# A fused attention and two-layer mixture kernel: the first block multiplies unsplit float32, the weights are split behind it, and the list scheduler models VectorE and GpSimd as alternating

## The chip, the core and the metric

The kernel runs on one core of a Trainium2 chip. The metric is device microseconds of one execution. The kernel before takes 977.46 us (median of 3 runs, 977.22 to 979.46).

## The reference

Three stages follow one another, with 4 sequences of 768 steps (3072 tokens of 384 channels, 8 heads of 48).

```python
# 1: gated linear attention, a recurrence over time with a complex decay
scale = np.minimum(mag, 0.999) / (mag + 1e-06)      # mag = |a|
new_re = ar * S_re - ai * S_im;  new_im = ar * S_im + ai * S_re
S_re, S_im = new_re + k[t] v[t]^T, new_im;  y[t] = q[t] @ S_re
# 2: x = (x @ w_a) * (x @ w_b) @ w_out              384 -> 1536 -> 384
# 3: the best of 8 experts per token: out = gate * (relu(x @ w1[e]) @ w2[e])
```

The weights `w_a`, `w_b` and `w_out` of stage 2 are stored as float64, 36 pieces of 128 x 384 values.

## The kernel before

The first two stages run over 12 blocks of 256 tokens, each with two halves c of 128. For a block, `pre` turns the decay into factors on k and q (elementwise on VectorE, ScalarE and GpSimd; DMAs then turn them into `kT` and `qT`), `attn` computes scores, mask, y and the running state with fp32 products, and `planned_moe` does stage 2. The experts of stage 3 follow in program order after block 11.

Stage 2 works in three passes of fp32r: each operand is split into a high part H (ScalarE's copy, which rounds) and a remainder L (a subtraction), and a product is the sum of H*H, H*L and L*H. For one of 12 slices f of 128 inner channels, `up(j, f)` does 18 matmuls of 256 columns into `ab_p`; `gate_a` and `gate_b` multiply both halves into `g`; `gate_H` (ScalarE) and `gate_L` (GpSimd) split it; `down(j, f)` adds six matmuls of 392 columns to `o` (384 channels and 8 gate columns that were folded into `w_out`: `turned`, `kept`, `folded`). `close` empties `o`, `store` writes it to memory.

Each piece of weights is unpacked by `conv`: a DMA loads 384 KB of float64 words; three integer operations on VectorE (`shift` L771, `low` L774, `sign` L777) put an fp32 value together from both words in `ca`; ScalarE makes H (`high` L784), GpSimd the remainder (`rest` L788). A load waits for the unpacking six pieces before (`AHEAD`). Blocks 0 and 1 need the weights while they are still being unpacked, so their stage 2 is cut in halves: block 0 with f 0 to 5, block 1 with f 0 to 5, block 0 with f 6 to 11, block 1 with f 6 to 11 (`HALVES`); the first half of each is kept in SBUF (`part`, `keep`) and added by `close`.

The order of all instructions of this part is the work of a list scheduler, `Plan`. `P.add` takes an engine, a duration (from `on`), what is read and written, and a due time `at`. `P.run` walks in model time: among the operations that could start first, the one with the lowest due time is issued. So a due time is a priority, and the engines then run their queues in the order written. The due times are in `PRE` (elementwise work of each block), `ATT`, `CONV` (start and step of the unpacking), `HALVES` and `SLOT` (49 for each later block). Which elementwise products go to GpSimd is in `ON_POOL`, by block (3 stands for all later ones). Before the change the model delays only a VectorE operation marked `fast`, and only behind a GpSimd operation. `spans` (in blocks 3 to 11, four pieces each) loads the weights again and checks their range.

Of the kernel before, what the change touches and what calls it, by code (L numbers as in the profile page):

```python
# [24 lines left out]
AHEAD = 6  # L25
# [265 lines left out]
class Plan:  # L291
# [5 lines left out]
    def add(self, engine, weight, f, r=(), w=(), at=0.0, take=None, give=None, size=0, fast=False, early=0.0, soft=None):  # L297
# [13 lines left out]
        self.ops.append(dict(e=engine, d=weight, f=f, at=at, need=need, take=take, give=give, size=size, fast=fast, early=early, soft=soft, n=n))  # L311
        return n

    def run(self):
# [13 lines left out]
        gone, pipe, port, out, sent = {}, 0.0, (0.0, 0.0), [], [0.0] * 8  # L328
        while any(open_.values()):
# [75 lines left out]
def fast(tc, q, k, v, a_re, a_im, w_a, w_b, w_out, w_gate, w1, w2, out, dram, x2d):  # L405
# [5 lines left out]
    with ExitStack() as mctx, ExitStack() as ctx:  # L411
# [89 lines left out]
        def spans(i, src, nm, f, at):  # L501
# [3 lines left out]
            def load():  # L505
                raw = G["r"] = cvp.tile([128, 2, DM + NE], U32, tag="part", name="ck", bufs=2).rearrange("p h n -> p (h n)")[:, 0:768].rearrange("p (n two) -> p n two", two=2)
# [8 lines left out]
            P.add("SP", 0.06, load, w=[("part", i % 2)], at=at, size=393, early=at)  # L515
            for n, op in enumerate((ALU.max, ALU.min)):
                P.add("DVE", on("DVE", 384), reduce(n, op), r=[("part", i % 2)], w=[("span", i, n)], at=at + 6)
# [230 lines left out]
        three = cvp.tile([128, 1], U32, name="three")  # L748
        nc.vector.memset(three, 3)

        def conv(i, f, src, nm, at):
# [4 lines left out]
            ca, bits = ("x2", i % 5) if x2 else ("ca", i % 5 if i % 5 else 2), ("bits", i)  # L756

            def load():
                raw = wts.tile([128, 768], U32, tag=f"w{nm}{f}", name="raw")
                if nm == "o":  # L760
                    d = nc.sync.dma_start(out=raw, in_=src[f * 128:(f + 1) * 128].bitcast(U32))
                else:
                    d = nc.sync.dma_start(out=raw.rearrange("p (k n) -> p k n", k=3), in_=src.bitcast(U32)[:, f * 256:(f + 1) * 256].rearrange("(k p) n -> p k n", p=128))
# [3 lines left out]
                K["lo"], K["hi"] = raw[:, :, 0], raw[:, :, 1]  # L767
# [8 lines left out]
            def sign():  # L776
                r = nc.vector.scalar_tensor_tensor(out=K["a"], in0=K["hi"], scalar=0xC0000000, in1=K["a"], op0=ALU.bitwise_and, op1=ALU.bitwise_or)  # L777
                unpacked[i] = getattr(r, "ins", r).name
                K["a"] = K["a"].bitcast(F32)
# [142 lines left out]
        def planned_moe(j, f0, f1, lo, hi, on_pool):  # L922
# [6 lines left out]
            def falls(f, at):  # L929
                P.add("PE", 1.08, lambda: down(j, f, f0, f1 - 1), r=[("gH", base + f), ("gL", base + f), ("W", "o", f), ("G", f)], w=["o0", "o1"], at=at)  # L930
                if f < f1 - 1:
                    return
# [498 lines left out]
```

## Time and profile before

| | kernel before |
|---|---|
| median of the runs | 977.46 us |
| the profiled execution | 977.4 us |
| its span (first to last instruction) | 975.6 us |
| mean granted clock of TensorE | 0.972 |
| TensorE, VectorE, ScalarE, GpSimd busy | 890.0, 632.1, 441.4, 383.3 us |

The page gives busy times over the whole span; the windows view cuts the span into stretches and gives for each the busy time of every engine and the granted clock. The lines view groups instructions by line and shape, with busy time and mean duration, and what ended the idle time before them. The timeline lists single instructions with their start. PE is TensorE, DVE is VectorE, ACT is ScalarE, POOL is GpSimd, SP issues the DMAs. Neighbouring rows of one engine overlap by up to about 0.1 us; the time from start to start is what an instruction costs its queue.

### The profile page before, as it was taken

What the parts mean: (1) busy time and instruction counts of PE and PEld (TensorE: products, weight loads), DVE (VectorE), ACT (ScalarE), POOL (GpSimd) and SP (SyncE); (2) the same over time, 40 slices, a digit from 0 to 9 for tenths busy, and PEclk for the clock granted to TensorE, in tenths of its full rate; (3) what the DMA queues carried; (4) which work ended last, traced back from release to release, by engine and by line L of the source; (5) the groups of instructions that cost most, each with busy time, mean ns of one, the idle gap of its engine ahead of it and who ended that gap; (6) DMA issues with size and microseconds to landing.
All of it is one profiled execution on the core that took longest, in us unless ns stands there. A gap on an engine that the chain in (4) does not pass through costs nothing. (4 is left out here: it accounts for less than half of the span.)

```text
span 975.6 us, 19062 instructions
## 1 busy us (share of the span) xinstructions
PE 890.0 (91%) x7404; PEld 863.2 (88%) x7404; DVE 632.1 (65%) x1222; ACT 441.4 (45%) x824; POOL 383.3 (39%) x364
## 2 busy tenths in 40 slices
PE   0467896898999999999999999999999999999994
PEld 0357886898999999999999999999999999999994
DVE  6988999696958585858585959433573455444540
ACT  5445444554645555545454545222443444343430
POOL 3634555633334343334343434121415363342411
PEclk9999698799999999999999999999999999999997
DMA  8561742337261625161626161302334354443611
GB/s 223 160 173 51 212 119 66 82 108 198 64 197 45 187 65 164 42 187 42 180 55 180 26 171 26 99 2 77 120 106 137 109 174 125 150 150 110 178 38 23
DMA packets 128897, 112.72 MB, mean 116 GB/s; under 512 B 36564, under 2 KB 123446, under 8 KB 128796
## 3 DMA queue, kind: packets, MB, share of 16 engines
q1 hardware_dynamic: 122620, 101.30, 36.7%
q0 software_dynamic: 6176, 10.08, 3.5%
q8 instruction: 61, 1.00, 0.4%
q14 instruction: 40, 0.33, 0.1%
HBM read 82.42 MB, written 10.56 MB: 95 GB/s over the span
## 5 line engine op out<-in xcount | busy, mean ns | idle before, releaser
L854 POOL TENSOR_TENSOR gL<-g,gH 128x256 fp32r<-128x256 f32 x132 | 112.9, 857 | 213.7 <-ACT gH L850 207.5
L838 PE MATMUL ab_p<-xH,wa 128*128 128x256 f32 x864 | 189.3, 295 | 4.9 <-DVE g L846 4.5
L838 PE MATMUL ab_p<-xH,wb 128*128 128x256 f32 x864 | 180.4, 285 | 0.0
L863 PE MATMUL o<-wo,gH 128*128 128x392 f32 x576 | 154.6, 349 | 5.3 <-ACT gH L850 5.3
L838 PEld LDWEIGHTS ab_p<-xH,wa 128*128 128x128 f32 x864 | 147.3, 195 | 9.0 <-DVE g L846 6.1
L838 PEld LDWEIGHTS ab_p<-xH,wb 128*128 128x128 f32 x864 | 146.9, 194 | 0.0
L843 ACT COPY g<-ab_p 128x256 f32<-128x256 f32 x144 | 53.2, 370 | 196.6 <-PE ab_p L838 189.9
L846 DVE TENSOR_TENSOR g<-g,ab_p 128x256 f32<-128x256 f32 x144 | 59.7, 414 | 117.9 <-ACT g L843 117.7
L838 PE MATMUL ab_p<-xL,wa 128*128 128x256 f32 x432 | 123.8, 286 | 2.8 <-DVE xL L1238 2.8
L838 PE MATMUL ab_p<-xL,wb 128*128 128x256 f32 x432 | 123.2, 285 | 0.0
L863 PEld LDWEIGHTS o<-wo,gH 128*128 128x128 f32 x576 | 98.7, 191 | 6.6 <-ACT gH L850 5.7
L863 PE MATMUL o<-wo,gL 128*128 128x392 f32 x288 | 99.9, 347 | 3.3 <-POOL gL L854 3.3
L710 DVE SCALAR_TENSOR_TENSOR hL<-h_p,hH 128x256 fp32r<-128x256 f32 (+5 forms) x80 | 41.3, 517 | 90.6 <-ACT hH L709 90.3
L838 PEld LDWEIGHTS ab_p<-xL,wa 128*128 128x128 f32 x432 | 84.4, 195 | 3.0 <-DVE xL L1238 3.0
L709 ACT ACTIVATE hH<-h_p 128x256 fp32r<-128x256 f32 (+5 forms) x80 | 36.7, 459 | 110.5 <-PE h_p L705 109.9
L838 PEld LDWEIGHTS ab_p<-xL,wb 128*128 128x128 f32 x432 | 84.0, 194 | 0.0
L850 ACT ACTIVATE gH<-g 128x256 fp32r<-128x256 f32 x144 | 59.5, 414 | 51.8 <-DVE g L846 51.7
L723 PE MATMUL o<-w2H,hH 128*128 128x384 f32 (+4 forms) x232 | 79.1, 341 | 0.0
L723 PE MATMUL o<-w2H,hL 128*128 128x384 f32 (+4 forms) x232 | 78.5, 338 | 0.0
L723 PE MATMUL o<-w2L,hH 128*128 128x384 f32 (+4 forms) x232 | 78.3, 338 | 0.0
L705 PE MATMUL h_p<-sH,w1H 128*128 128x256 f32 (+5 forms) x240 | 77.4, 322 | 0.0
L705 PE MATMUL h_p<-sH,w1L 128*128 128x256 f32 (+5 forms) x240 | 76.9, 320 | 0.0
(192 smaller groups left out, 1979.2 us busy)
## 6 DMA issues: line engine op xcount, KB each, us to landing
raw<-in_moe_w_dram SPq DMA_DIRECT2D x64, 384.0 KB, 3.5
q<-in_q_dram SPq DMA_DIRECT2D x24, 192.0 KB, 3.4
v<-in_v_dram SPq DMA_DIRECT2D x24, 192.0 KB, 3.3
raw<-in_moe_w_a_dram SPq DMA_DIRECT2D x12, 384.0 KB, 3.9
raw<-in_moe_w_b_dram SPq DMA_DIRECT2D x12, 384.0 KB, 5.0
raw<-in_moe_w_out_dram SPq DMA_DIRECT2D x12, 384.0 KB, 3.5
x2d<-x SPq DMA_DIRECT2D x24, 192.0 KB, 2.7
ck<-in_moe_w_a_dram SPq DMA_DIRECT2D x12, 384.0 KB, 3.3
```

Of the source, the lines that this page charges most:

```text
L705: nc.tensor.matmul(out=t, lhsT=lh[:, o:o + 128], rhs=rh[:, kk].rearrange("p c t -> p (c t)"), start=n == 0, stop=n == 8)
L709: nc.scalar.activation(out=hH, in_=t, func=ACTF.Relu)
L710: nc.vector.scalar_tensor_tensor(out=hL, in0=t, scalar=0.0, in1=hH.bitcast(F32), op0=ALU.max, op1=ALU.subtract)
L723: nc.tensor.matmul(out=G["o", c], lhsT=lh[:, c * r:(c + 1) * r], rhs=rh, start=f == 0 and n == 0, stop=f == NH - 1 and n == 2)
L838: nc.tensor.matmul(out=t[:, i], lhsT=lh[:, kk * 128:(kk + 1) * 128], rhs=rh[:, kk], start=n == 0, stop=n == 8)
L843: nc.scalar.copy(out=G["g", j, f], in_=G["ab", j, f][:, 0])
L846: nc.vector.tensor_tensor(out=G["g", j, f], in0=G["g", j, f], in1=G["ab", j, f][:, 1], op=ALU.mult)
L850: nc.scalar.activation(out=G["H", j, f], in_=G["g", j, f], func=ACTF.Copy)
L854: eng.tensor_tensor(out=G["L", j, f], in0=G["g", j, f], in1=G["H", j, f].bitcast(F32), op=ALU.subtract)
L863: nc.tensor.matmul(out=G["o", j, c], lhsT=lh[:, c * C:(c + 1) * C], rhs=rh, start=f == first and n == 0, stop=f == last and n == 2)
```

## The change

Block 0 is no longer split. Its attention output is copied as fp32 (`x32`), `up32` multiplies it with the unpacked weights `A32` (6 fp32 matmuls of 256 columns for a slice), the gate is one product without H and L, and `down32` does two fp32 matmuls of 392 columns. `conv` stops after `sign`, which writes the value over the high word of the loaded piece (so values lie two words apart); `shift` is a tensor_scalar with an immediate. `parted` splits the pieces afterwards, with `high` on ScalarE and `rest` on VectorE, due from 84 at steps of 1.2. Each piece is loaded into the place of the tile that the next one's split will take (`follows`), so a split waits until the piece in its place has been split. Blocks 0 and 1 run whole and one after the other (`M0`, `M1`), and `part` is gone; block 1's `gate_L` is on VectorE. Fewer elementwise products are on GpSimd, and where `sq` isn't, the square is on ScalarE. The scheduler's `lock` marks operations of VectorE and GpSimd that take turns: one that would start while the other engine's last is running ends after it by its own duration. `alone=False` exempts those that read PSUM and some others. Loads go 14 pieces ahead, with earliest times in `LOAD`. The range checks are in the last six blocks, six pieces each.

```diff
-AHEAD = 6
+AHEAD = 14
+LOAD = (4.0,2.0,7,30.0,2.0)
...
-PRE = ((0.0, 24.0), (10.0, 34.0), (28.0, 52.0), (100.0, 132.0), (140.0, 176.0))
-ATT = (36.0, 54.0, 124.0, 145.0)
-CONV = (30.0, 2.4)
-HALVES = ((44.0, 72.0), (72.0, 96.0), (96.0, 118.0), (118.0, 138.0))
+PRE = ((0.0, 20.0), (2.0, 22.0), (40.0, 70.0), (100.0, 125.0), (140.0, 166.0))
+ATT = (26,66,110,156)
+CONV = (22,1.8)
+M0 = (40.0, 90.0)
+M1 = 88
+SPLIT = (84,1.2)
...
 ON_POOL = {
     0: ("sq", "add", "imul", "k1", "q1"),
-    1: ("sq", "add", "imul", "kA", "qA", "k1"),
-    2: ("sq", "add", "imul", "kA", "qA", "q1"),
-    3: ("sq", "add", "qA", "q1"),
+    1: ("x",),
+    2: ("qA", "q1"),
+    3: ("add", "qA", "q1"),
 }
+GL_POOL = (2, 12)
+L_POOL = ()
...
-            if o["fast"] and x < port[1]:
-                x = port[1]
             end = x + o["d"]
-            if e == "POOL" and o["d"] > 0.3:
-                port = (x, end)
-            free[e] = end
+            if o["lock"]:
+                if port[0] != e and port[1] > x:
+                    end = port[1] + o["d"] - (0.13 if e == "DVE" else 0.06)
+                port = (e, end)
+            free[e] = end - (0.075 if e == "DVE" and o["d"] > 0.2 else 0.0)
...
-            P.add("SP", 0.06, load, w=[("part", i % 2)], at=at, size=393, early=at)
+            P.add("SP", 0.06, load, w=[("s", "bo"[i % 2], NF)], at=at, size=393, early=at)
...
+        follows = {("a", f): ("b", f) for f in range(NF)}
+        follows.update({("b", f): ("a", f + 1) for f in range(NF - 1)})
+        follows.update({("o", f): ("o", f + 1) for f in range(NF - 1)})
+        A32 = {}
...
+            to = follows.get((nm, f))
+            slot = ("s",) + (to or (nm, NF))
+
+            start = LOAD[0] + LOAD[1] * i if i < LOAD[2] else LOAD[3] + LOAD[4] * (i - LOAD[2])
...
-                raw = wts.tile([128, 768], U32, tag=f"w{nm}{f}", name="raw")
+                raw = wts.tile([128, 2 * n], U32, tag="w%s%d" % to, name="raw") if to else cvp.tile([128, 2 * n], U32, tag="last" + nm, name="raw")
...
+                K["lo"], K["hi"] = raw[:, 0:384, 0], raw[:, 0:384, 1]
+                A32[nm, f] = raw[:, :, 1].bitcast(F32)
...
-                nc.vector.scalar_tensor_tensor(out=K["a"], in0=K["hi"], scalar=0x07FFFFFF, in1=three.to_broadcast([128, 384]), op0=ALU.bitwise_and, op1=ALU.logical_shift_left)
+                nc.vector.tensor_scalar(out=K["a"], in0=K["hi"], scalar1=0x07FFFFFF, scalar2=3, op0=ALU.bitwise_and, op1=ALU.logical_shift_left)
...
-                r = nc.vector.scalar_tensor_tensor(out=K["a"], in0=K["hi"], scalar=0xC0000000, in1=K["a"], op0=ALU.bitwise_and, op1=ALU.bitwise_or)
+                r = nc.vector.scalar_tensor_tensor(out=K["hi"], in0=K["hi"], scalar=0xC0000000, in1=K["a"], op0=ALU.bitwise_and, op1=ALU.bitwise_or)
...
-            def high():
-                w = wts.tile([128, 2, n], F32R, tag=f"w{nm}{f}", name=f"w{nm}{f}")
-                W[nm, f] = w[:, 0], w[:, 1]
-                nc.scalar.activation(out=w[:, 0, 0:384], in_=K["a"], func=ACTF.Copy)
...
-            def rest():
-                wH, wL = W[nm, f]
-                nc.gpsimd.tensor_tensor(out=wL[:, 0:384], in0=K["a"], in1=wH[:, 0:384].bitcast(F32), op=ALU.subtract)
...
-            P.add("SP", 0.06, load, r=[("bits", i - AHEAD)], w=[("raw", i)], at=at - 14, size=393)
-            P.add("DVE", on("DVE", 384), shift, r=[("raw", i)], w=[ca, "next"], at=at)
-            P.add("DVE", on("DVE", 384), low, r=[("raw", i), ca], w=[ca], at=at)
-            P.add("DVE", on("DVE", 384), sign, r=[("raw", i)], w=[ca, bits], at=at)
-            P.add("ACT", on("ACT", 384), high, r=[ca], w=[("H", nm, f)], at=at)
-            P.add("POOL", on("POOL", 384), rest, r=[ca, ("H", nm, f)], w=[("W", nm, f)], at=at)
+
+            P.add("SP", 0.06, load, r=[("bits", i - AHEAD)], w=[slot], at=start, early=start, size=393)
+            P.add("DVE", on("DVE", 384, fast=True), shift, r=[slot], w=[ca], at=at)
+            P.add("DVE", on("DVE", 384), low, r=[slot, ca], w=[ca], at=at)
+            P.add("DVE", on("DVE", 384), sign, r=[ca], w=[slot, bits, ("A32", nm, f)], at=at)
...
+            def beside():
+                nc.scalar.copy(out=A32[nm, f][:, DM:DM + NE], in_=K["t"])
...
+            P.add("ACT", 0.17, beside, r=[("wg_p", f)], w=[("A32", nm, f)], at=at + 3, give=t)
...
+        def parted(i, f, nm, at):
+
+            n = 384 + (NE if nm == "o" else 0)
+            slot, mine = ("s",) + follows.get((nm, f), (nm, NF)), ("s", nm, f)
+
+            def high():
+                w = wts.tile([128, 2, n], F32R, tag=f"w{nm}{f}", name=f"w{nm}{f}")
+                W[nm, f] = w[:, 0], w[:, 1]
+                nc.scalar.activation(out=w[:, 0], in_=A32[nm, f], func=ACTF.Copy)
+
+            e = "POOL" if i in L_POOL else "DVE"
+
+            def rest():
+                wH, wL = W[nm, f]
+                (nc.gpsimd if e == "POOL" else nc.vector).tensor_tensor(out=wL, in0=A32[nm, f], in1=wH.bitcast(F32), op=ALU.subtract)
+
+            P.add("ACT", on("ACT", n), high, r=[slot, ("A32", nm, f)], w=[mine, ("H", nm, f)], at=at)
+            P.add(e, on(e, n), rest, r=[slot, ("A32", nm, f), ("H", nm, f)], w=[("W", nm, f)], at=at)
...
+        def up32(f):
+            t = G["ab", 0, f] = p_ab.tile([128, 2, BT], F32, tag="ab", name="ab_p")
+            for i, nm in enumerate("ab"):
+                for kk in range(3):
+                    nc.tensor.matmul(out=t[:, i], lhsT=A32[nm, f][:, kk * 128:(kk + 1) * 128], rhs=xT["F", 0][:, kk].rearrange("p c t -> p (c t)"), start=kk == 0, stop=kk == 2)
+
+        def down32(f):
+            for c in range(2):
+                if f == 0:
+                    G["o", 0, c] = p_o.tile([128, DM + NE], F32, tag=f"o{c}", name=f"o{c}")
+                nc.tensor.matmul(out=G["o", 0, c], lhsT=G["g", 0, f][:, c * C:(c + 1) * C], rhs=A32["o", f], start=f == 0, stop=f == NF - 1)
...
+        def planned_moe(j, lo, hi):
+            step = (hi - lo) / (NF + 1)
+            at = lo
...
+                if j:
+                    P.add("PE", 1.08, lambda: down(j, f, 0, NF - 1), r=[("gH", j * NF + f), ("gL", j * NF + f), ("W", "o", f)], w=["o0", "o1"], at=at)
+                else:
+                    P.add("PE", 1.38, lambda: down32(f), r=[("gL", f), ("A32", "o", f), ("s",) + follows.get(("o", f), ("o", NF))], w=["o0", "o1"], at=at)
...
+                if j == 0:
+                    P.add("PE", 2.6, lambda f=f: up32(f), r=[("x", 0)] + [x for nm in "ab" for x in (("A32", nm, f), ("s",) + follows.get((nm, f), (nm, NF)))], w=[a], at=at)
+                    P.add("ACT", on("ACT", BT, True), lambda f=f: gate_a(j, f), r=[a], w=[("gL", n), ("gL", n - 3)], at=at)
+                    P.add("DVE", on("DVE", BT), lambda f=f: gate_b(j, f), r=[a], w=[("gL", n)], at=at, alone=False)
+                else:
+                    P.add("PE", 2.12, lambda f=f: up(j, f), r=[("x", j % 2), ("W", "a", f), ("W", "b", f)], w=[a], at=at)
+                    P.add("ACT", on("ACT", BT, True), lambda f=f: gate_a(j, f), r=[a], w=[g], at=at)
+                    P.add("DVE", on("DVE", BT), lambda f=f: gate_b(j, f), r=[a, g], w=[g], at=at, alone=False)
+
+                    P.add("ACT", on("ACT", BT), lambda f=f: gate_H(j, f), r=[g], w=[("gH", n), ("gH", n - 3)], at=at)
+                    e = "POOL" if GL_POOL[0] <= j < GL_POOL[1] else "DVE"
+                    P.add(e, on(e, BT), lambda f=f, e=e: gate_L(j, f, nc.gpsimd if e == "POOL" else nc.vector), r=[g, ("gH", n)], w=[("gL", n), ("gL", n - 3)], at=at)
...
+                if "sq" in ON_POOL[min(j, 3)]:
+                    nc.gpsimd.tensor_tensor(out=T("Bt"), in0=L("im"), in1=L("im"), op=ALU.mult)
+                else:
+                    nc.scalar.activation(out=T("Bt"), in_=L("im"), func=ACTF.Square)
...
+                def x32(c=c, S=S):
+                    if c == 0:
+                        xT["F", 0] = mo.tile([128, 3, 2, C], F32, tag="cc", name="x", bufs=4)
+                    nc.scalar.copy(out=xT["F", 0][:, :, c], in_=S["y"])
...
+                if j:
+                    add("ACT", on("ACT", 384, True), xH, ["y"], [("xH", j % 2)] + ([("x", j % 2)] if c == 0 else []))
+                    add("DVE", on("DVE", 384), xL, ["y", ("xH", j % 2)], [("x", j % 2)], alone=False)
+                else:
+                    add("ACT", on("ACT", 384, True), x32, ["y"], [("x", 0)])
...
-            return HALVES[3][1] + (j - 3) * SLOT
+            return M1 + (j - 2) * SLOT
...
-                for (b, f0, f1), (lo, hi) in zip(((0, 0, NF // 2), (1, 0, NF // 2), (0, NF // 2, NF), (1, NF // 2, NF)), HALVES):
-                    planned_moe(b, f0, f1, lo, hi, True)
+                planned_moe(0, *M0)
+                for i, (f, _, nm) in enumerate(pieces):
+                    parted(i, f, nm, SPLIT[0] + i * SPLIT[1])
                 continue
             lo = begin(j)
-            if j > 2:
-                planned_moe(j - 1, 0, NF, lo, lo + SLOT, True)
+            planned_moe(j - 1, lo, lo + SLOT)
...
-                for i, (f, src, nm) in list(enumerate(pieces))[n:n + 4]:
-                    spans(i, src, nm, f, lo + 4 + (i - n) * 10)
+            P.add("POOL", 2.4, scatter, r=["posu"], w=["tab"], at=at + 4, alone=False)
+            if j >= NB - 6:
+                n = (j - NB + 6) * 6
+                for i, (f, src, nm) in list(enumerate(pieces))[n:n + 6]:
+                    spans(i, src, nm, f, lo + 2 + (i - n) * 7)
```

## Rows read from the trace of the kernel before

**Rows 1.** The page's busy times, shares of the span and instructions of each engine

```profile
PE 890.0 (91%) x7404; PEld 863.2 (88%) x7404; DVE 632.1 (65%) x1222; ACT 441.4 (45%) x824; POOL 383.3 (39%) x364
```

**Rows 2.** Windows: busy time by engine, granted clock, DMA share and GB/s of each stretch

```profile
22.00:182.00 160.00, 114.65 (x832) 104.97 (x833) 145.03 (x223) 70.83 (x140) 84.45 (x63) 0.87 0.42 119
...
230.00:960.00 730.00, 728.98 (x6134) 714.09 (x6135) 431.93 (x874) 330.37 (x616) 266.21 (x255) 1.00 0.39 112
```

**Rows 3.** Timeline of TensorE (start, duration, operation), its last stall before block 2

```profile
230.17 0.38 PE L838 MATMUL ab_p<-xL,wa 128*128 128x256 f32 x1 [2.77 <-DVE xL L1238]
```

**Rows 4.** Waits of TensorE, 30 to 182 us: total, times, longest

```profile
PE wt_p L803 <- DVE ca L777: 44.7, 5, 34.6
```

**Rows 5.** Lines of VectorE, 22 to 182 us (busy us, mean ns): the unpacking

```profile
L777 DVE SCALAR_TENSOR_TENSOR ca<-raw,ca 128x384 uint32<-128x384 uint32 x36 | 33.6, 933 | 0.1
L771 DVE SCALAR_TENSOR_TENSOR ca<-raw,three 128x384 uint32<-128x384 uint32 x36 | 29.0, 804 | 0.0
L774 DVE SCALAR_TENSOR_TENSOR ca<-raw,ca 128x384 uint32<-128x384 uint32 x36 | 27.8, 772 | 0.2
```

**Rows 6.** Lines of GpSimd, the same stretch

```profile
L788 POOL TENSOR_TENSOR wa<-ca,wa 128x384 fp32r<-128x384 f32 x12 | 15.5, 1294 | 21.9 <-ACT wa L784 20.9 <-ACT wo L815 1.1
...
L788 POOL TENSOR_TENSOR wo<-ca,wo 128x384 fp32r<-128x384 f32 x12 | 14.8, 1236 | 8.1 <-ACT wo L784 8.1
L854 POOL TENSOR_TENSOR gL<-g,gH 128x256 fp32r<-128x256 f32 x12 | 12.6, 1052 | 9.8 <-ACT gH L850 9.2 <-DMA raw<-in_moe_w_a_dram 0.4
...
L1034 POOL TENSOR_TENSOR q<-q,A 128x768 f32<-128x768 f32 x2 | 4.1, 2038 | 1.6 <-DVE A L1070 1.6
```

**Rows 7.** Timeline of VectorE, 97.8 to 101.4 us

```profile
97.83 0.55 DVE L771 SCALAR_TENSOR_TENSOR ca<-raw,three 128x384 uint32<-128x384 uint32 x1
98.30 1.35 DVE L777 SCALAR_TENSOR_TENSOR ca<-raw,ca 128x384 uint32<-128x384 uint32 x1
99.57 1.82 DVE L774 SCALAR_TENSOR_TENSOR ca<-raw,ca 128x384 uint32<-128x384 uint32 x1
```

**Rows 8.** Timeline of GpSimd, the same moment

```profile
98.07 1.16 POOL L788 TENSOR_TENSOR wb<-ca,wb 128x384 fp32r<-128x384 f32 x1 [1.05 <-ACT wb L784]
99.20 1.78 POOL L1057 TENSOR_TENSOR Bt<-im 128x768 f32<-128x768 f32 x1
```

**Rows 9.** Timeline of VectorE elsewhere: a fast and a plain operation

```profile
24.64 0.42 DVE L1112 TENSOR_SCALAR X<-X 128x384 f32<-128x384 f32 x1
...
92.14 0.94 DVE L1128 TENSOR_TENSOR Bt<-k,X 128x768 f32<-128x768 f32 x1
```

**Rows 10.** Timeline of TensorE at full clock, 119 to 136 us

```profile
119.26 2.02 PE L1190 MATMUL sc_p<-qT,kT 96*128 96x128 f32 x16
121.11 0.94 PE L1199 MATMUL kn_p<-ident,kT 96*128 96x96 f32 x8
...
123.08 0.43 PE L1229 MATMUL y_p<-sm,v 128*32 128x128 f32 x8
...
124.98 1.56 PE L1243 MATMUL kv_p<-v,kn 128*96 128x48 f32 x16
126.37 0.84 PE L803 MATMUL wt_p<-ident,ca 128*128 128x128 f32 x6
...
129.17 0.73 PE L812 MATMUL wg_p<-wg,wt 128*128 128x8 f32 x6
129.76 0.36 PE L838 MATMUL ab_p<-xH,wa 128*128 128x256 f32 x1
...
134.12 0.53 PE L863 MATMUL o<-wo,gH 128*128 128x392 f32 x2
...
135.19 0.73 PE L812 MATMUL wg_p<-wg,wt 128*128 128x8 f32 x6
```

**Rows 11.** Timeline of TensorE at low clock, the first scores

```profile
38.78 3.76 PE L1190 MATMUL sc_p<-qT,kT 96*128 96x128 f32 x16
```

**Rows 12.** Lines of ScalarE, 22 to 182 us: the high part

```profile
L784 ACT ACTIVATE wa<-ca 128x384 fp32r<-128x384 f32 x12 | 6.3, 522 | 10.4 <-DVE ca L777 10.4
```

More of the change, by code (lines that the diff above doesn't have):

```diff
@@ L295, in __init__, with add @@
         self.ops, self.wrote, self.read, self.rings = [], {}, {}, rings
-    def add(self, engine, weight, f, r=(), w=(), at=0.0, take=None, give=None, size=0, fast=False, early=0.0, soft=None):
+    def add(self, engine, weight, f, r=(), w=(), at=0.0, take=None, give=None, size=0, early=0.0, soft=None, alone=True):
         n = len(self.ops)
@@ L310, in add @@
         need.discard(n)
-        self.ops.append(dict(e=engine, d=weight, f=f, at=at, need=need, take=take, give=give, size=size, fast=fast, early=early, soft=soft, n=n))
+        self.ops.append(dict(e=engine, d=weight, f=f, at=at, need=need, take=take, give=give, size=size, early=early, soft=soft, lock=alone and engine in ("DVE", "POOL"), n=n))
         return n
@@ L505, in load @@
             def load():
-                raw = G["r"] = cvp.tile([128, 2, DM + NE], U32, tag="part", name="ck", bufs=2).rearrange("p h n -> p (h n)")[:, 0:768].rearrange("p (n two) -> p n two", two=2)
+                raw = G["r"] = cvp.tile([128, 2 * (384 + (0, NE)[i % 2])], U32, tag="last" + "bo"[i % 2], name="ck")[:, 0:768].rearrange("p (n two) -> p n two", two=2)
                 if nm == "o":
@@ L863, in down @@
                     nc.tensor.matmul(out=G["o", j, c], lhsT=lh[:, c * C:(c + 1) * C], rhs=rh, start=f == first and n == 0, stop=f == last and n == 2)
-        def keep(j, c):
-            if c == 0:
-                G["part", j] = cvp.tile([128, 2, DM + NE], F32, tag="part", name="part", bufs=2)
-            nc.scalar.copy(out=G["part", j][:, c], in_=G["o", j, c])
         def close(j, c):
-            o, part = G["o", j, c], G["part", j][:, c] if ("part", j) in G else None
+            o = G["o", j, c]
             x2 = mo.tile([128, DM], F32, tag="x2", name="x2", bufs=2)
@@ L932, in falls @@
                     return
                 for c in range(2):
-                    if half:
-                        P.add("ACT", on("ACT", DM + NE, True), lambda c=c: keep(j, c), r=[f"o{c}"], w=[("part", j)] if c == 0 else [("part", j, 1)], at=at)
-                    else:
-                        P.add("ACT" if whole and c == 0 else "DVE", on("DVE", DM) + 0.16, lambda c=c: close(j, c), r=[f"o{c}", ("part", j), ("part", j, 1)] + ([("lgt", j % 2, 0)] if c else []), w=[("x2", c), ("lgt", j % 2, c)], at=at)
-                        P.add("SP", 0.06, lambda c=c: store(j, c), r=[("x2", c)], at=at, size=196)
@@ L1086, in pre @@
             add("ACT", sq_re, ks("re"), new("A", "Cc", "F"))
-            add(pick("sq")[0], sq_im, ks("im"), new("Bt"))
+            add("POOL" if "sq" in ON_POOL[min(j, 3)] else "ACT", sq_im, ks("im"), new("Bt"))
             act("Cc", "A", ACTF.Ln, bias=tiny)
@@ L1100, in pre @@
             add("DVE", lambda: nc.vector.tensor_scalar(out=T("Cc"), in0=T("Cc"), scalar1=MAX_TAN, scalar2=-MAX_TAN, op0=ALU.min, op1=ALU.max), ks("Cc"), ks("Cc"), fast=True)
-            add("DVE", low, ks("A"), [("low", jf)], weight=0.16)
+            add("DVE", low, ks("A"), [("low", jf)], weight=0.16, alone=False)
             act("Bt", "A", ACTF.Ln, bias=tiny)
             act("Bt", "Bt", ACTF.Exp, scale=-1.0)
-            add("DVE", most, ks("Cc"), [("most", jf)])
+            add("DVE", most, ks("Cc"), [("most", jf)], alone=False)
             one = len(todo)
@@ L1143, in mul @@
                     for x in "Aq":
-                        add("DVE", column(x), ks("A", x), [("column", x)], weight=0.16)
+                        add("DVE", column(x), ks("A", x), [("column", x, lo)], weight=0.16)
                 add(e, times, ks(src, "Cc" if c2 == 0 else "F"), ks(t))
@@ L1147, in mul @@
                     first = c2 == 0 and lo == 0 and jj == 0
-                    add("SP", turn(jj), ks(t) + [("column", t)] + ([] if first else ks(src + "T")), (every(src + "T") if first else []) + [(src + "T", c, c2, jj) for c in cs], size=65 * n, key=src if first else None, soft=src)
+                    add("SP", turn(jj), ks(t) + [("column", t, lo)] + ([] if first else ks(src + "T")), (every(src + "T") if first else []) + [(src + "T", c, c2, jj) for c in cs], size=65 * n, key=src if first else None, soft=src)
             mul("k", 0, C)
@@ L1161, in pre @@
                 elif weight is None:
-                    weight = on(e, m, fast=kw.get("fast", False)) if e == "DVE" else on(e, m, bias=bias) if e == "ACT" else on(e, m)
+                    weight = on(e, m, fast=kw.pop("fast", False)) if e == "DVE" else on(e, m, bias=bias) if e == "ACT" else on(e, m)
                 key, kw["soft"] = kw.pop("key", None), made.get((kw.get("soft"), j))
```

68 lines of the change are left out of this document (18 added, 50 removed).

## The prediction

> **What bounds the kernel now.** I read the busy shares of the page first: TensorE is busy for 91% of the span, VectorE for 65% [rows 1]. That average hides two stages, so the windows view comes next [rows 2]. From 230 to 960 us TensorE is busy 728.98 of 730 us, at the full clock: nothing done to VectorE there can show. From 22 to 182 us it is the other way round: VectorE is busy 145 of 160 us, TensorE 115, at a mean granted clock of 0.87. The timeline of TensorE says where one stage ends: its last stall, 2.77 us for the x of block 2, ends at 230.17 [rows 3], with the first product of block 2 behind it. So the run is a head of 230.2 us and a tail of 975.6 - 230.2 = 745.4 us in which TensorE sets the pace.
>
> The waits of TensorE in the head name the supplier: 44.7 us in five waits for `ca`, the weights that VectorE unpacks (34.6 of them before its first instruction) [rows 4]. By lines, the three unpacking operations take 33.6 + 29.0 + 27.8 = 90.4 us there, 36 of each, means 933, 804 and 772 ns [rows 5]. Left alone one takes 0.55 us, and the next starts 0.47 us after it; beside a GpSimd product it takes 1.35 or 1.82 us [rows 7], and ends 0.4 us or so after the product does [rows 8]: 98.30 + 1.35 = 99.65 against 98.07 + 1.16 = 99.23. The two engines take turns on such operations, and the time of the head is the sum of both. GpSimd runs three groups of twelve weight remainders there, 14.8 to 15.5 us each, and 12 `gL` at 1.05 us, 12.6 us [rows 6].
>
> **The change part by part: VectorE's path.** What must be done on VectorE and GpSimd between 22.2 us, where unpacking begins, and the start of block 2, at the spacing of undisturbed operations:
> - Unpacking: the second and third operations keep 0.47 each. The first becomes a tensor_scalar on uint32 with a stride, which no row shows: 0.47 if it stays as it is, 0.34 if it runs as the fp32 tensor_scalar of 384 columns does (0.42 long, less 0.08 of overlap) [rows 9]. So 1.28 to 1.41 for a weight, 46 to 51 us for 36; I take 48.
> - The rest of block 0's elementwise work: about a dozen operations at 0.47 and four GpSimd products of 1.1, 10 us (an estimate).
> - Block 1's elementwise work, now all on VectorE but for a square on ScalarE: fifteen operations of 768 columns at 0.87 (0.94 less the overlap) [rows 9], nine scans counted as five more, three fast ones at 0.47, 0.4 of small ones: 19. Block 2's: the same, but two products go to GpSimd at 2.04 [rows 6]: 21.
> - Masks and states of attention for blocks 0, 1, 2: four masks of 0.6 and up to six operations of 0.47 each, 13 in all. Gates: 12 for block 0, 24 for block 1 (its `gL` moves from GpSimd to VectorE), each 0.33: 12. Closing and routing: 3.
> - Added: 36 remainders of the split, now on VectorE, 36 x 0.47 = 17.
>
> The sum is 48 + 10 + 19 + 21 + 13 + 12 + 3 + 17 = 143. VectorE was idle 15 of 160 us (9%) with a backlog all the while [rows 2]; with that share again, 143 / 0.906 = 158, and block 2 could start at 22 + 158 = 180. What goes is the collision: of the 90.4 us of unpacking, 108 x 0.55 = 59 are its own and 31 were waits for GpSimd.
>
> The Trainium skill, "VectorE: DVE Perf Modes", section "What auto-detection actually checks", has a single-source operation run two elements a cycle if it lies in SBUF and its outer size is even, whatever its type. By it the shift would be the fast one, and the sum 3 us shorter (an estimate).
>
> **TensorE's path.** The unsplit block costs more. An fp32 product of 128 columns takes (121.11 - 119.26) / 8 = 0.231 us, each recorded as two matmuls [rows 10]. 256 columns are at most 0.46, and at least four times 256 columns at 2.4 GHz, 0.43: I take 0.45, and 0.68 for 392 columns. `up32` is then 6 x 0.45 = 2.7 and `down32` 2 x 0.68 = 1.36; twelve of both, 48.7 us. In three passes it is (134.12 - 129.76) / 2 = 2.18 and 135.19 - 134.12 = 1.07 [rows 10]: 39 us. So the block costs 9.7 us more, and what it buys is that it waits for unpacking alone. Its weights are read with a stride of two words. The nearest rows are VectorE's, which reads them so at the 0.55 of dense operands; I take nothing for it, and up to 16 us if the twelve `down32` take double.
>
> One c of attention is 1.85 for the scores, 0.94 at most for the transposes, 1.90 (y) and 1.39 (kv): 6.1 [rows 10]; half of y falls away at the start of a sequence, kv and transposes at its end. Blocks 0, 1, 2 make 11 + 12 + 10. Folding the gate weights is 0.42 + 0.59 for each of 12: 12. With both blocks' products: 11 + 12 + 10 + 12 + 48.7 + 39 = 133 us at full clock. The first scores begin at 38.8 at half speed, 3.76 instead of 2.02 us [rows 11], so 172 is the floor. I add 7 for some 15 us of work at the low clock until the dense products come, and 5 for gaps between attention's two halves in block 0: 184.
>
> Both paths end close together, and what is late next is whichever is later: 184. Behind it the tail is the same work in the same order, TensorE full; the square moved to ScalarE, the remainders left on GpSimd and the range checks packed into six blocks lie in the 298 idle us (VectorE's) or more that each other engine has there [rows 2]. If that cover failed, the cost would be stalls that TensorE doesn't have now. Loads: 36 of 384 KB are wanted in about 90 us, and SP's queue issues them in its order between the transposing DMAs; the DMA engines are 42% busy there at 119 GB/s [rows 2], so I charge nothing, and leave it to the range.
>
> The span becomes 975.6 - (230.2 - 184) = 929.4. The profiled execution took 977.4, 1.8 more than its span, and stands at the median of the runs (977.46): **931 us**, 921 to 943 for starts of block 2 from 174 to 196.
>
> **The rivals.**
> - Neither path loses to the other: no idle share, the shift fast, the clock up from the first dense product. VectorE then ends at 22 + 141 = 163, TensorE at its floor less the 3 us by which block 0's second half is due earlier: 169, so 916. For it: a full TensorE keeps its clock for 730 us [rows 2]. Against: every wait in the head so far [rows 4].
> - The chain of splits binds. A split tile lies where the weight before it was unpacked, so each waits for the remainder before: ScalarE's copy, 0.52 [rows 12], then 0.47 on VectorE. Where a remainder stands at the head of VectorE's queue before its copy is done, everything behind it waits, about 0.6 us in 36 cases: 22 us, block 2 at 206, 953. For it: the same pair made GpSimd wait 20.9 us for `wa` in the head [rows 6]. Against: GpSimd had nothing else to do then.
> - Slower: the unsplit block stays at the low clock. Scores, folds and transposes kept TensorE at half speed [rows 11]; if the fp32 products of block 0 do too, TensorE needs 2 x (11 + 12 + 12 + 48.7) = 167 us for what lies ahead of block 1, until 206, and 49 more: 255, so 1002. It is slower than now from a loss of 46 us on, so only if nearly all of block 0 runs so. For it: rows 11. Against: these are short and thin tiles with waits between. The Trainium skill, "TensorE: Matmul & The Clock Gate", section "What's actually happening", has sustained activity release the clock, whatever the type; by it this rival would not come, and no run here shows an unsplit 128-row product yet.
> - The change doesn't do what it says: the head is held by loads and SP's order, block 2 starts near 230, 975 to 980.
>
> **How the numbers follow.** The forecast gets 0.53, the faster rival 0.17, the chain of splits 0.20, the low clock 0.06, no effect 0.03; 0.01 is for a tail with new stalls. I count as a change what differs by over 0.3%, 2.9 us. Faster is 0.53 + 0.17 + 0.20 = 0.90, the same 0.03, slower 0.07. A range of 905 to 962 holds the forecast whole, all of the faster rival and over half of the slower chain: 0.8.
>
> **What would show it.** Right: the first product of block 2 near 184 and TensorE without stalls behind it; unpacking at 0.55 us with no stretch while GpSimd rests; `up32` records of 0.22 us spacing at full clock; VectorE busy over 85% until 150 or so. Wrong: waits of TensorE for `wL` (the chain), a granted clock of 0.5 through block 0, waits of VectorE for raw weights, or a tail that is not 745 us.

## The result and the profile after

The changed kernel took **935.38 us**, the median of four runs (935.16 to 938.14), beside 977.81 for the kernel before on the same chip: a ratio of 0.957, 95% interval 0.9548 to 0.9591. The forecast was 931. The profiled execution has a span of 933.3 us.

The page's line of busy times, which answers to [rows 1]:

```profile
PE 871.8 (93%) x7308; PEld 840.8 (90%) x7308; DVE 606.6 (65%) x1261; ACT 446.4 (48%) x821; POOL 288.8 (31%) x285
```

VectorE's share is what it was. The windows (length, then busy time and instructions of each engine, granted clock, DMA share, GB/s) say where the time went, as [rows 2] did before:

```profile
22.00:182.00 160.00, 138.40 (x1149) 122.90 (x1153) 144.79 (x316) 87.75 (x165) 15.10 (x10) 0.99 0.48 142
182.00:230.00 48.00, 45.88 (x392) 44.97 (x385) 39.38 (x71) 31.83 (x53) 19.07 (x17) 0.96 0.31 88
230.00:920.00 690.00, 687.49 (x5777) 672.94 (x5776) 407.11 (x832) 313.19 (x582) 245.07 (x233) 1.00 0.41 115
```

In the same 160 us TensorE does 138 us of work instead of 115, at 0.99 of its clock instead of 0.87. VectorE is as busy as before, but gets 316 instructions done instead of 223. GpSimd has 15 us of work left there instead of 84. The tail is as full as it was. The timeline of TensorE shows the end of the head, which stood at 230.17 [rows 3]. There `xL`, the remainder of block 2's input, comes in; the products with its high part `xH` start a little earlier:

```profile
184.13 0.39 PE L852 MATMUL ab_p<-xH,wa 128*128 128x256 f32 x1 [0.71 <-ACT xH L1259]
185.43 0.42 PE L852 MATMUL ab_p<-xL,wa 128*128 128x256 f32 x1 [0.92 <-DVE xL L1262]
185.66 0.63 PE L852 MATMUL ab_p<-xH,wa 128*128 128x256 f32 x2
```

By `xL` block 2 starts at 185.4 us, 44.7 earlier; its very first product, with `xH`, stands at 184.1 instead of 227.0. For head and tail I count from `xL`, as the prediction did. The tail is 933.3 - 185.4 = 747.9 us, 2.5 more than before. So the whole gain comes from the head. The waits of TensorE from 30 to 182 us (total, times, longest) have lost the later stalls for unpacked weights that [rows 4] had; the one that is left is the start:

```profile
PE wt_p L803 <- DVE raw L789: 33.5, 1, 33.5
PE sc_p L1209 <- DMA qT<-q: 4.9, 1, 4.9
PE wg_p L812 <- ACT wt L807: 1.8, 3, 0.6
```

The unpacking and the remainders by lines of VectorE, 22 to 182 us (busy us, mean ns | idle ahead), to be held against [rows 5, 6]:

```profile
L789 DVE SCALAR_TENSOR_TENSOR raw<-raw,ca 128x384 uint32<-128x384 uint32 x36 | 20.5, 576 | 0.0
L786 DVE SCALAR_TENSOR_TENSOR ca<-raw,ca 128x384 uint32<-128x384 uint32 x36 | 19.6, 552 | 0.0
L783 DVE TENSOR_SCALAR ca<-raw 128x384 uint32<-128x384 uint32 x36 | 13.9, 395 | 0.0
...
L836 DVE TENSOR_TENSOR wo<-raw,wo 128x392 fp32r<-128x392 f32 x12 | 6.8, 563 | 0.6 <-ACT wo L830 0.5
```

90.4 us of unpacking became 54.0. To see what that is made of, I take for each form of instruction the duration that only a tenth of its records stay under as its own time, and call what a record has beyond it stretch. From 22 us to the start of block 2 VectorE's time divides so (own time less the overlap of neighbours, which closes the sum):

| | own work | stretch | idle | together |
|---|---|---|---|---|
| before, to 230.2 | 132.0 | 53.7 | 22.5 | 208.2 |
| after, to 185.4 | 138.4 | 9.6 | 15.4 | 163.4 |

VectorE took over work and lost 44 us of stretch. Before, all but about 1 us of the stretch fell on records beside which a GpSimd operation ran. That is bookkeeping of two traces; it does not say yet which part of the change bought it.

### The profile page after: what moved, and what is told of

Its sections match the earlier page's. It is cut to its first block, busy times and chain, and to the rows that moved or that the text cites. A ratio compares the mean times of both kernels' runs of the same rounds, so it can differ in the third digit from the quotient of the medians.

```text
span 933.3 us, 18743 instructions
## 1 busy us (share of the span) xinstructions
PE 871.8 (93%) x7308; PEld 840.8 (90%) x7308; DVE 606.6 (65%) x1261; ACT 446.4 (48%) x821; POOL 288.8 (31%) x285
## 5 line engine op out<-in xcount | busy, mean ns | idle before, releaser
L852 PE MATMUL ab_p<-xH,wa 128*128 128x256 f32 x792 | 168.3, 289 | 0.7 <-ACT xH L1259 0.7
L852 PE MATMUL ab_p<-xH,wb 128*128 128x256 f32 x792 | 162.6, 282 | 0.0
L880 POOL TENSOR_TENSOR gL<-g,gH 128x256 fp32r<-128x256 f32 x108 | 94.8, 878 | 218.6 <-ACT gH L876 206.0
L869 ACT COPY g<-ab_p 128x256 f32<-128x256 f32 x144 | 53.5, 372 | 190.9 <-PE ab_p L852 168.9
L889 PE MATMUL o<-wo,gH 128*128 128x392 f32 x528 | 139.7, 345 | 0.0
L852 PEld LDWEIGHTS ab_p<-xH,wa 128*128 128x128 f32 x792 | 131.4, 189 | 3.1 <-issue 2.1
L852 PEld LDWEIGHTS ab_p<-xH,wb 128*128 128x128 f32 x792 | 131.7, 190 | 0.0
L852 PE MATMUL ab_p<-xL,wa 128*128 128x256 f32 x396 | 111.5, 282 | 1.2 <-DVE xL L1262 1.2
L852 PE MATMUL ab_p<-xL,wb 128*128 128x256 f32 x396 | 111.6, 282 | 0.0
L889 PE MATMUL o<-wo,gL 128*128 128x392 f32 x264 | 90.1, 341 | 0.0
L710 PE MATMUL h_p<-sL,w1H 128*128 128x256 f32 (+5 forms) x240 | 76.8, 320 | 0.0
```

The costliest lines, as they stand in the source:

```text
L710: nc.tensor.matmul(out=t, lhsT=lh[:, o:o + 128], rhs=rh[:, kk].rearrange("p c t -> p (c t)"), start=n == 0, stop=n == 8)
L852: nc.tensor.matmul(out=t[:, i], lhsT=lh[:, kk * 128:(kk + 1) * 128], rhs=rh[:, kk], start=n == 0, stop=n == 8)
L869: nc.scalar.copy(out=G["g", j, f], in_=G["ab", j, f][:, 0])
L880: eng.tensor_tensor(out=G["L", j, f], in0=G["g", j, f], in1=G["H", j, f].bitcast(F32), op=ALU.subtract)
L889: nc.tensor.matmul(out=G["o", j, c], lhsT=lh[:, c * C:(c + 1) * C], rhs=rh, start=f == first and n == 0, stop=f == last and n == 2)
```

## The experiments

Theory at the start: the head has two paths that end close together, and the collisions of VectorE with GpSimd were the larger part of the gain. Rivals: the planner's better model of the engines, the loads, or TensorE alone. The planner's two kernels, block 0 in three passes and the remainders on VectorE in the kernel before ran on a chip where the kernel before takes 986.94 us, the others where it takes 976.9 to 978.5. So ratios are compared, and "us" below is the ratio times 977.8; the change itself stands at 935.8 so. By the intervals, the difference of two rows is uncertain by 3 to 5 us. The last column has the product with `xH`.

| kernel | ratio, 95% interval | us | first product of block 2 |
|---|---|---|---|
| the change | 0.957 (0.9548 to 0.9591) | 935.8 | 184 |
| planner without alternation | 0.9575 (0.9543 to 0.9607) | 936.2 | 187 |
| before, planner with alternation | 1.0041 (1.0015 to 1.0068) | 981.8 | 226 |
| block 0 in three passes | 0.9689 (0.9655 to 0.9723) | 947.4 | 198 |
| products on GpSimd | 0.9674 (0.963 to 0.9717) | 945.9 | 196 |
| remainders on GpSimd | 0.9646 (0.9613 to 0.9678) | 943.2 | 192 |
| loads as before | 0.9617 (0.96 to 0.9634) | 940.3 | 187 |
| slow shift | 0.9604 (0.9588 to 0.9621) | 939.1 | 188 |
| products and remainders on GpSimd | 0.9711 (0.9686 to 0.9735) | 949.5 | 200 |
| before, remainders on VectorE | 0.9969 (0.9948 to 0.999) | 974.8 | 224 |
| less TensorE work | 0.9573 (0.954 to 0.9605) | 936.0 | 186 |
| less VectorE work | 0.9514 (0.9483 to 0.9545) | 930.3 | 178 |
| less of both | 0.9483 (0.9467 to 0.9499) | 927.2 | 173 |

Most rows hold one thing more than their name says: where an edit changes an operation's engine, its duration or when a load may start, the planner writes another order. Only "less TensorE work" keeps the change's order on VectorE (all 364 operations up to 186 us), and "less of both" keeps that of "less VectorE work".

**The planner's model, taken out and put in alone.** In the changed kernel:

```
-  self.ops.append(dict(..., lock=alone and engine in ("DVE", "POOL"), n=n))
+  self.ops.append(dict(..., lock=False, n=n))
```

> The changed kernel, but its scheduler does not model that VectorE and GpSimd take turns; all instructions are the same, only their order can differ. Theory (the 42 us come from work taken off the sum of VectorE and GpSimd in the head, and 10 GpSimd operations are left there): block 2 starts within 6 us of 185.4, time 933 to 941. Rival (the order that the model finds is what gains): a good part of the 42 us is lost again, 950 to 975.

Measured 944.32, a ratio of 0.9575: the change's. The other way round the kernel before got the new `Plan.run` and its `alone` flags, nothing else:

> The kernel before with only the scheduler's new model of alternation, its due times and engines as they were. Theory: the sum of VectorE and GpSimd in the head stays, so 965 to 980. Rival (order): 940 to 955.

Measured 989.15, 1.0041: if anything slower. A part of the change, the scheduler's model of the two engines as alternating, buys nothing that shows, with the new work or without it.

**Block 0 in three passes.** The unsplit slices become none; weights are split ahead of block 0 as they come:

```
-SPLIT = (84,1.2)
+SPLIT = (25,1.8)
+K0 = 0
...
-                if j == 0:
+                if j == 0 and f < K0:
...
```

> The changed kernel with block 0 in three passes again: each piece is split as soon as it is unpacked (due from 25 at steps of 1.8), remainders on VectorE; all else as changed. Ahead of block 0's end VectorE has 36 x 0.47 + 12 x 0.4 = 22 us more to do, TensorE 9 us less over both blocks. Theory (both paths are close, leaving the splits for later buys some of VectorE's time): block 2 at 187 to 197, 937 to 947. Rival A (the unsplit block is the heart of the gain): 955 to 975. Rival B (TensorE alone sets the head now): 9 us less than the change, 926.

Measured 955.95, 0.9689, which is 947.4 where the kernel before takes 977.8: 12 us of the 42, at the far end of the 937 to 947 that the theory gave. Its windows show how it loses:

```profile
22.00:182.00 160.00, 124.89 (x1041) 117.77 (x1042) 139.57 (x303) 86.34 (x168) 12.80 (x9) 0.91 0.45 133
```

TensorE has less to do and is further behind: idle for 20 us from 40 us to the first product of block 2 (7 in the change), at 0.91 of its clock. With remainders between a weight and its product TensorE stands more often: each of its three longest stalls (3.59, 3.99 and 3.30 us, between 70 and 106 us) was followed by work at 1.2 GHz.

**Work put back on GpSimd, the products, the remainders, both.**

```
 ON_POOL = {
-    1: ("x",),
-    2: ("qA", "q1"),
-    3: ("add", "qA", "q1"),
+    1: ("sq", "add", "imul", "kA", "qA", "k1"),
+    2: ("sq", "add", "imul", "kA", "qA", "q1"),
+    3: ("sq", "add", "qA", "q1"),
```

> The changed kernel with the elementwise products on GpSimd as before (six for block 1, six for block 2, four for later blocks, the square among them). By the prediction's durations VectorE and GpSimd together get 6.5 + 4.6 = 11 us more to do in the head. Theory (TensorE sets the head, VectorE is close behind): 938 to 946. Rival A (no bound is touched): 934 to 937. Rival B (this is where the unexplained 27 us of the gain lie): 955 to 965.

```
-L_POOL = ()
+L_POOL = tuple(range(36))
```

> The changed kernel with the 36 remainders of the split on GpSimd again. The run with the remainders moved in the kernel before showed that one on GpSimd had cost VectorE about 0.64 us of stretch, against 0.47 on VectorE itself. Theory (TensorE sets the head, the remainders lie beside it, but the chain from split to split grows by 0.7 us a link): 938 to 947. Rival A (they don't matter): 933 to 937. Rival B (VectorE pays their whole time, as the prediction's sum has it): 36 x 0.78 = 28 us more, 960 to 965.

945.88 (0.9674) and 941.99 (0.9646): 10 and 7.4 us, both within what the theory gave. Together, which leaves the unsplit block, the shift, the loads and the due times of the change:

> The changed kernel with both the 36 remainders and the former elementwise products back on GpSimd, so that what is left of the change is the unsplit first block, the fast shift, the due times and the planner's model. Alone the two cost about 7.5 and 10 us. Theory A (the parts add): 950 to 956 on a chip where the kernel before takes 977, that is 0.972 to 0.978 of it. Theory B (the parts work only together, since GpSimd's operations stretch VectorE's that fall beside them and either set fills the time with them): 960 to 968. If one covers the other: 944 to 948.

Measured 949.45, 0.9711: 13.7 us for both, between "they add" (17.5) and "one covers the other". The unpacking lines of that kernel show the collisions come back at once:

```profile
L789 DVE SCALAR_TENSOR_TENSOR raw<-raw,ca 128x384 uint32<-128x384 uint32 x36 | 26.7, 747 | 0.0
L786 DVE SCALAR_TENSOR_TENSOR ca<-raw,ca 128x384 uint32<-128x384 uint32 x36 | 26.0, 727 | 0.0
L783 DVE TENSOR_SCALAR ca<-raw 128x384 uint32<-128x384 uint32 x36 | 18.9, 534 | 0.0
```

0.75, 0.73 and 0.53 us instead of 0.58, 0.55 and 0.40: 17.6 us more for the same 108 operations.

**The collision alone, in the kernel before.** If a GpSimd product costs VectorE its whole length, moving 36 weight remainders and the 24 `gL` of blocks 0 and 1 to VectorE must pay by itself:

```
-                nc.gpsimd.tensor_tensor(out=wL[:, 0:384], ...
+                nc.vector.tensor_tensor(out=wL[:, 0:384], ...
...
-            P.add("POOL", on("POOL", 384), rest, ...
+            P.add("DVE", on("DVE", 384), rest, ...
...
-                    planned_moe(b, f0, f1, lo, hi, True)
+                    planned_moe(b, f0, f1, lo, hi, False)
```

> The kernel before with the 36 weight remainders and the 24 gL of blocks 0 and 1 moved from GpSimd to VectorE, nothing else. In the head the sum of both engines falls by about 36 x (1.25 - 0.47) + 12 x (1.05 - 0.33) = 37 us. Theory (the collision is the cost): 942 to 956. Rival A (unsplit block): at most 10 us, 967 to 978.

Measured 984.1, 0.9969: 3 us, where 21 to 35 were expected. The theory fell; the rival's range (at most 10 us) held. Its unpacking lines and its window:

```profile
L774 DVE SCALAR_TENSOR_TENSOR ca<-raw,ca 128x384 uint32<-128x384 uint32 x36 | 22.1, 614 | 0.1
L777 DVE SCALAR_TENSOR_TENSOR ca<-raw,ca 128x384 uint32<-128x384 uint32 x36 | 21.6, 600 | 0.0
L771 DVE SCALAR_TENSOR_TENSOR ca<-raw,three 128x384 uint32<-128x384 uint32 x36 | 21.3, 592 | 0.0
```

```profile
22.00:182.00 160.00, 113.03 (x853) 102.04 (x854) 138.73 (x276) 74.30 (x146) 26.47 (x15) 0.81 0.42 120
```

The collisions did go: 65 us of unpacking instead of 90.4. By the same division as above, to 226 us, VectorE's stretch fell from 53.7 to 19.8, but its own work rose from 132 to 155 and its idle time from 22.5 to 28.9. TensorE did no more than before, at a clock of 0.81. So a moved operation saved VectorE some 34/60 = 0.6 us and cost it 23/60 = 0.4; of the 11 us between, 6 went into longer waits. In that kernel each remainder stands ahead of products of block 0; in the change it is made later, and there the place of the 36 remainders alone is worth 7.4 us. That their place in the order makes this difference is not shown: no run changes the order alone, and the two kernels differ in more than that.

**Which path sets the head.** Two kernels leave work of one path out: the products of `w_b` in the unsplit block sum over one of three groups of channels,

```
-                for kk in range(3):
+                m = 3 if nm == "a" else 1
+                for kk in range(m):
...
```

> The changed kernel with two of the three products of w_b left out in each of block 0's twelve slices: TensorE has 24 x 0.43 = 10.4 us less to do ahead of block 1, every other engine the same. Times for a chip on which the kernel before takes 977.5 and the changed one 935.4. Theory (TensorE now sets the head): 8 to 11 us less, 924 to 928. Rival (VectorE still sets it): 932 to 936.

and the low words of the weights are left out,

```
-            P.add("DVE", on("DVE", 384), low, r=[slot, ca], w=[ca], at=at)
```

> The changed kernel without the second unpacking operation (the low bits of every weight stay zero): VectorE has 36 x 0.47 = 17 us less to do, all of it ahead of block 0's end. Times as on a chip with 977.5 before. Theory (TensorE sets the head): at most 4 us less, 931 to 936. Rival (VectorE sets it): 12 to 17 us less, 918 to 923. If both take turns, half of it.

935.87 (0.9573) and 929.69 (0.9514). Ten us less for TensorE are worth nothing, against the 8 to 11 expected; 17 less for VectorE are worth 5.5, between the theory's 4 at most and the rival's 12 to 17. The windows, the first kernel's and then the second's:

```profile
22.00:182.00 160.00, 132.78 (x1047) 116.32 (x1048) 142.72 (x308) 85.52 (x163) 13.52 (x9) 0.96 0.48 141
```

```profile
22.00:182.00 160.00, 140.02 (x1177) 124.99 (x1178) 135.33 (x292) 91.32 (x170) 13.79 (x10) 1.00 0.49 146
```

With less to do TensorE is idle longer, 12.8 us from 40 us to the first product of block 2 instead of 7.1, and its clock falls to half twice there, from 54.3 and from 115.7 us, instead of once. Its busy time falls from 137.0 to 133.6 us only: of the 10.4 us that it was spared 7 come back as slower work and 6 as waits. Its timeline has one set of score products ahead of such a stretch and the next one in it:

```profile
120.36 3.75 PE L1210 MATMUL sc_p<-qT,kT 96*128 96x128 f32 x16
```

The set at 109.50 took 1.95. With less for VectorE TensorE is idle for 5.2 us only and keeps its clock. I read this as VectorE's list a little the later and TensorE close behind it. It is a reading: the clock took its part in the first kernel, and the second one's order is another. If it holds, both cuts at once must pay what one did not:

> The changed kernel with both reductions at once: two of the three products of each w_b slice in the unsplit block left out (10.4 us of TensorE; that part of the reference isn't computed) and no instruction for the low three bits of each weight word (17 us of VectorE; those bits are zero). Alone the first gave 0 and the second 5.5 us. Theory (two paths of nearly equal length end together at the start of block 2): with VectorE lightened TensorE sets the end, so its 10.4 us now come out nearly whole: 919 to 925, start of block 2 at 168 to 173. Rival (a third chain, of the attention and the elementwise work of block 1 or of the loads, holds what is left): 928 to 931, the same as without the low words alone.

Measured 927.65, 0.9483, 927.2 on the scale of the table: 8.6 us better than the change, 3.1 better than VectorE's cut alone. That lies between the ranges of the theory (919 to 925) and of the rival (928 to 931). Block 2's first product stands at 173.0, as the theory said, 5.3 us earlier than with VectorE's cut alone, whose order this kernel shares. The time does not follow as far: from the first product on the run takes 751.9 us, 2.7 more than the change (749.2). The windows of the later stretches show TensorE standing where it did not:

```profile
190.00:230.00 40.00, 38.88 (x383) 37.39 (x382) 30.66 (x61) 22.62 (x41) 16.48 (x14) 1.00 0.33 78
...
500.00:700.00 200.00, 197.88 (x1767) 194.32 (x1767) 110.56 (x269) 79.71 (x164) 61.47 (x70) 1.00 0.35 102
```

In the change these are 40.00 and 199.84. So a head that ends earlier seems to take slack out of the blocks behind it. Of 10.4 us of TensorE 5.3 came out in the head; its idle time there, from 40 us on, was 8.5 us, most of it for folds of the gate weights, mask products and a transfer (none above 2.5 us). Which chain these belong to I did not settle.

**The loads and the shift.**

```
-AHEAD = 14
+AHEAD = 6
-  P.add("SP", 0.06, load, ..., at=start, early=start, size=393)
+  P.add("SP", 0.06, load, ..., at=at - 14, size=393)
```

> The changed kernel with the loads of the weights as before: at most 6 slices ahead of the unpacking instead of 14, and each due 14 us before its unpacking. Where the single undone parts measured so far add up to about 30 of the 42 us, some 12 us are not assigned. Theory (VectorE works through its list without waiting for loads: in the profile of the change its waits from 40 to 135 us are for TensorE and ScalarE, none of them for a transfer): 933 to 938, the same as the change. Rival (the loads 14 ahead carry part of the unassigned 12 us): 941 to 947, with VectorE waiting for transfers of raw weights in the trace.

940.58, 0.9617: 4.5 us, outside the theory's range and just short of the rival's, but not for the rival's reason. VectorE's waits (20 to 185 us):

```profile
DVE g L872 <- ACT g L869: 8.1, 7, 4.8
DVE sm L1213 <- PE sc_p L1209: 3.8, 3, 2.3
DVE ca L783 <- DMA raw<-in_moe_w_out_dram: 0.4, 1, 0.4
```

Raw weights are waited for 0.4 us. What grew is the wait for block 1's gates, 2.2 us in the change. The unpacking ends at 124.6 us instead of 129.5, but block 2 starts 2.7 us later: with other load times the planner wrote another order, and a worse one: from the 82nd operation of VectorE on the two differ.

```
-  nc.vector.tensor_scalar(out=K["a"], in0=K["hi"], scalar1=0x07FFFFFF, scalar2=3, ...)
+  nc.vector.scalar_tensor_tensor(out=K["a"], in0=K["hi"], scalar=0x07FFFFFF, in1=three.to_broadcast([128, 384]), ...)
```

> The changed kernel with the shift of the unpacking written as before: scalar_tensor_tensor with a broadcast tile of threes instead of tensor_scalar with two immediates. In the traces the first takes 0.47 us undisturbed and 0.77 with what GpSimd cost it, the second 0.39: 36 times 0.08 to 0.18 is 3 to 6.5 us more on VectorE's path. Theory (both paths close, VectorE's a little the longer): 937 to 941. Rival (the planner's order has slack enough for it): 934 to 936. If the shift were most of the unassigned 12 us, 945 or more.

939.42, 0.9604: 3.3 us. The line takes 20.9 us instead of 13.9, so about half of what VectorE pays reaches the end, if the new order that comes with it is worth nothing.

**What the parts are worth.** Undone one at a time: unsplit block 11.6, products 10.1, remainders 7.4, loads 4.5, shift 3.3, the planner's model 0.4 (nothing that can be told from zero). Together 37 of 42. Since pairs need not add (13.7 for 17.5), these are prices in the presence of the rest, each with the order that the planner wrote for it, not shares. The due times and the packing of the range checks were not tried alone.

## Why the prediction was right, point by point

**The head and the tail.** Block 2 was forecast for 184 and came at 185.4; the tail for 745.4, and was 747.9. Of the 2.5 us, 1.5 are the first 53 products of block 2, which ran at 1.2 GHz from 185.6 to 189.1 after the waits just ahead (8.07 us; the same 53 took 6.54 in the kernel before and 6.46 in the one with less of both, where the clock held). TensorE was idle 2.5 of 690 us later instead of 1.0 of 730, which makes up the rest and a little more. So 931 was 4.4 us short, within the forecast's own 921 to 943.

**VectorE's terms.** By the sums VectorE allowed block 2 at 180; the run's own sum is 138.4 of own work, 9.6 of stretch and 15.4 idle, 163.4 us from 22 on, which gives 185. The forecast's 143 was not all VectorE's: it counts six GpSimd products at their full length, 4 x 1.1 + 2 x 2.04 = 8.5 us, and so 134.5 of own work. The term that was short is own work, by 3.9 us; the price of what stayed on GpSimd (8.5 against 9.6 of stretch, about two thirds of that beside a GpSimd operation) and the idle share nearly held. About a third of the stretch is in the unpacking and the remainders, so it has not gone with ten GpSimd operations left. The fast shift makes the sum 2 us shorter (143 to 141), not 3. It took 0.395 a time, near the 0.42 of the fast row, and 0.591 undone, which costs 7.0 us of VectorE. The rule in the Trainium skill, "VectorE: DVE Perf Modes", "What auto-detection actually checks", that an operation with a single source in SBUF can run two elements a cycle, agrees.

**TensorE's terms.** `up32` is 2.59 us (2.7), two products of `down32` 1.39 (1.36), in the timeline by the starts of consecutive groups:

```profile
57.04 2.76 PE L859 MATMUL ab_p<-x,raw 128*128 128x256 f32 x12
59.63 0.73 PE L812 MATMUL wg_p<-wg,wt 128*128 128x8 f32 x6
...
70.48 1.54 PE L865 MATMUL o<-raw,g 128*128 128x392 f32 x4
71.87 1.46 PE L859 MATMUL ab_p<-x,raw 128*128 128x256 f32 x6
```

2.59 / 6 = 0.432 is the lower bound that the prediction gave, so no cost of the stride of two words in the weights shows, and the 16 us held in reserve for it were not needed. The low clock was put at 7 us of loss and the gaps at 5. They came to 4 and 9: the first scores began 2.6 us later, after 4.9 us for `qT`, and gaps took 6.7 from there to 185.4; but the clock rose to 2.4 GHz at 45.7 us, in block 0's first attention and long before the dense products that I had waited for, and fell once, for 3.4 us from 114, behind this stall:

```profile
113.74 0.74 PE L1218 MATMUL kn_p<-ident,kT 96*128 96x96 f32 x4 [1.68 <-DVE sm L1213]
114.41 0.66 PE L1248 MATMUL y_p<-sm,v 128*32 128x128 f32 x8
```

The sum held because two errors nearly cancelled, 13 in place of 12; what is left, 133.5 us of work at the full clock, is the forecast's 133. The rival "the unsplit block stays at the low clock" did not come: all 144 records of `up32`, from 57.0 to 130.8 us, took 0.38 to 0.47 us, and none lies in the stretch at 1.2 GHz. The rule in the Trainium skill, "TensorE: Matmul & The Clock Gate", "What's actually happening", that activity releases the clock, agrees.

**What was wrong in the working.** Two steps. "The two engines take turns on such operations, and the time of the head is the sum of both" prices a GpSimd operation at its length. By the trace before, 80 of them, 105 us long, stretched VectorE by 53.7, about half; and in the kernel before, where that rule gave 21 to 35 us, moving 60 of them to VectorE gave 3. In the forecast's own sum little hung on it, the 8.5 us of six products; the rest was priced as left alone. The other step: "what is late next is whichever is later: 184", with TensorE as the later. TensorE spared of 10.4 us gave nothing; VectorE spared of 17 gave 5.5; block 2's first product came 2 us later, 6 earlier, and with both spared 11 earlier. That the larger of 180 and 184 came so near is in part luck: VectorE's sum, with its own work right, gives about 184 by itself. The two paths are not two sums side by side. They feed each other (weights one way, scores and gate products the other), and one can inherit the other's gap; for TensorE a gap can cost clock as well. The rival "chain of splits" did not come in the change: remainders ran from 46.6 to 168.9 us, mostly behind their unpacking, and VectorE waited for ScalarE's copies 0.5 us in all. With block 0 in three passes, where the split stands ahead of the products, 12 us were lost; how much of it is this chain is not shown.

## To carry to other kernels

Moving an operation off an engine that collides pays for what the collision costs less what the work costs on its new engine. That can be near zero: here 3 us for 60 operations where the first block waits for the remainders, and 7.4 for the 36 remainders where it doesn't. Where a planner orders the work, an experiment on one part measures the new order too. Where two engines feed each other in turn, take work from each alone and then from both before naming the bound. And a stage that is cut short gives something back in the next, in slack and in clock: of 11 us in the head 8.6 arrived.

## What was not expected of the hardware

The granted clock rose to 2.4 GHz at 45.7 us, while TensorE was in block 0's first attention, whose fp32 scores had begun at 41.3. The profile of the kernel before shows it from 81.6 us on, but with the planner alone changed that kernel had it at 43 us too, for 10 us. So I don't credit the unsplit block with the early rise; what the change has is that it then holds but for one stretch, with 7 us of gaps instead of 31 from 40 us to the first product of block 2. Stalls of 1.68 and 0.92 us in the change were followed within a microsecond by 3.4 us at 1.2 GHz; in the kernel with less of both, stalls of 1.18 and 1.44 us were not, nor were 1.96 and 2.02 us in the kernel planned without alternation; and with less TensorE work the clock fell at 54.3 us with no stall above 0.6 us in the 12 us before. What tells them apart stays open.
